# Weight masks between decode steps, earlier exponentials and a regrouped last ten pairs in a convolution and two gated MLPs

## Chip, cores and metric

One core of one Trainium2 chip runs the whole program in one launch. The metric is device microseconds of one execution, lower is better. Before the change the median of 3 executions was 1251.18 us (1250.5 to 1252.2).

## What is computed

The reference, cut to what matters (8192 tokens, width 192, hidden widths 1536 and 2048, all in float32 accuracy):

```python
w = exp(weight_gen - max) / (sum + 1e-9)             # softmax over 7 taps, 8 heads per token
out = einsum('bshk,bskhg->bshg', w, x_unf)           # causal convolution with 7 taps
xn = out / sqrt(mean(out**2) + 1e-6) * rms_g
g = xn @ w_gate                                      # 192 x 1536
y = (g * sigmoid(g) * (xn @ w_val)) @ w_out          # 1536 x 192
h = y @ w_in                                         # 192 x 2048
z = (h * sigmoid(1.702 * h)) @ w_out2                # 2048 x 192
```

## The kernel before, in words

The tokens lie in 16 blocks of 512. Every product is made in three passes, since each operand is split into a high part `h` and a low rest `l` (both fp32r): high by high, high by low, low by high. The matrix rows are cut into an upper and a lower half of 64; two matmuls, one on each half of TensorE, run beside each other as a **pair** (`mm`, L376). Two halves may not write the same bank of PSUM in turn without a hand-over: `handed` (L389) puts a GpSimd nop between them, which waits for the one and is waited for by the other.

The work is a list of **units** (L544). A unit of kind 1, (1, b, m), makes the 128 hidden columns m of the first MLP for block b: `U1` (L455) sends pg and pv through TensorE (9 pairs), then ScalarE makes p = silu(pg) (L463), VectorE p = p * pv (L467), ScalarE h = high part of p (L468), VectorE l = p - h (L471). A unit of kind 2, (2, b, i), makes two slices of the second MLP (`U2`, L474): ScalarE h and p (L484, L485), VectorE l (L491). The down products of a unit (5 pairs per slice, `D1`, `D2`) are put one or two units later, so that h and l are there (`pend`). Four PSUM banks (`pu`) hold pg, pv and ph: a unit can only begin to fill a bank when the unit two before it has been read out of it. Blocks 0 and 1 go first, interleaved, then block by block; the first four units of kind 1 of the next block stand ahead of the eight units of kind 2 of this one. `Y` (L504) splits the first MLP's output for the second, `Z` (L524) scales the sums of the second and stores them.

Beside the units three side works run:

- **Pieces of weights.** 34 pieces (12 w1, 6 wo1, 8 w2, 8 wo2) arrive as 64-bit doubles, each loaded twice (`st`, and `zt` shifted by 16 bits; L87, L88; three buffers of each) and turned into high and low parts by `piece` (L82): x1 on ScalarE (L95), x2 on VectorE: two masks (L99 of st, L101 of zt), then x3, x4, x5 on VectorE (L105, L109, L115), each reading what the one before wrote, then x6, the high part, on ScalarE (L120). `piece_steps` (L592), called 33 times, moves a line of three pieces on: it ends the oldest, does x3 to x5 of the second and x1 and x2 of the third. x5 also calls `load_pieces`, which issues the loads of the piece after next.
- **Softmax.** Seven groups of blocks. `softmax_ops` (L162) gives VectorE operations ahead of the exponential (`pre`), one ScalarE exponential (L186; it needs a table load ahead of it and one behind it, back to silu), and VectorE operations behind it (`post`).
- **Convolution** of a block (`conv_ops`, L216): 13 VectorE operations of 768 columns and some small ones.

The order on every engine is that in which this program calls the operations (a manual schedule); `some` spreads the side works between the units by their estimated cost and due position. Where each group's exponential stands is set at L714 to L727: for group 3 at pos[2, nxt - 2, 2], the third unit of kind 2 of a block, for groups 4 to 6 two units behind `start_at`, that is among units of kind 1. The last two slices' down products (ten pairs) come after the last unit, one slice after the other (L763).

Of the kernel before, what the change touches and what calls it, by code (L numbers as in the profile page):

```python
# [9 lines left out]
F32 = mybir.dt.float32  # L10
# [4 lines left out]
ALU = mybir.AluOpType  # L15
# [3 lines left out]
P = 128  # L19
# [6 lines left out]
DR = D - P  # L26
# [4 lines left out]
BLOCKS = [4] * 16  # L31
# [6 lines left out]
TURN = 5  # L38
SIG = 1.702
# [3 lines left out]
def gated_conv_mlp(ctx: ExitStack, tc: tile.TileContext, xp, wg, w1, wo1, w2, wo2, g, out):  # L43
    nc = tc.nc
    NB = len(BLOCKS)
    T0 = [sum(BLOCKS[:i]) for i in range(NB)]
    TM = max(BLOCKS)
    NM = TM * P
# [33 lines left out]
    def piece(src, high, low):  # L82

        st = stg.tile([P, PC, 2], I32, tag="st", name="st")
        zt = stg.tile([P, PC + 1, 2], I32, tag="zt", name="zt")
        I16 = mybir.dt.int16
        nc.sync.dma_start(out=st.rearrange("p n t -> p (n t)"), in_=src.bitcast(I32))  # L87
        nc.sync.dma_start(out=zt.rearrange("p n t -> p (n t)").bitcast(I16)[:, 1:4 * PC + 1], in_=src.bitcast(I16))  # L88
        t = {}
        hi, mid = st[:, :, 1], zt[:, 0:PC, 1]  # L90

        def x1():
            t["a"] = dec.tile([P, PC], F32, tag="a", name="dec_a")

            nc.scalar.mul(out=t["a"], in_=hi.bitcast(F32), mul=2.0 ** -112)  # L95

        def x2():
            t["s"] = dec.tile([P, PC], I32, tag="s", name="dec_s")
            nc.vector.tensor_scalar(out=t["s"], in0=hi, scalar1=-0x80000000, scalar2=4,  # L99
                                    op0=ALU.bitwise_and, op1=ALU.bitwise_or)  # L100
            nc.vector.tensor_single_scalar(mid, mid, 7, op=ALU.logical_shift_left)  # L101

        def x3():
            ai = t["a"].bitcast(I32)
            nc.vector.scalar_tensor_tensor(out=ai, in0=ai, scalar=3, in1=t["s"],  # L105
                                           op0=ALU.logical_shift_left, op1=ALU.bitwise_or)

        def x4():
            nc.vector.tensor_single_scalar(t["s"], t["a"].bitcast(I32), -0x800000, op=ALU.bitwise_and)  # L109

        def x5():
            v, sf = mid, t["s"].bitcast(F32)
            if len(low.shape) == 3:
                v, sf = (x.rearrange("p (k d) -> p k d", d=D) for x in (v, sf))
            nc.vector.scalar_tensor_tensor(out=low, in0=v, scalar=2.0 ** -43, in1=sf, op0=ALU.mult, op1=ALU.mult)  # L115
            load_pieces()

        def x6():
            for out, of in high:
                nc.scalar.copy(out, of(t["a"]))  # L120
        return [x1, x2], [x3, x4, x5], [x6]

    def piece_up(src, i, nm):

# [251 lines left out]
    def mm(ps, N, rows, w, x, start, stop):  # L376
        def f():
            ins = nc.tensor.matmul(ps[:, :N], w[rows], x[rows, :N], start=start, stop=stop)  # L378
            handed(ins, ps, rows)
        return f  # L380
# [71 lines left out]
            g()  # L452


    def U1(b, m, todo):  # L455
        N = BLOCKS[b] * P
        pg = pu.tile([P, NM], F32, tag="u", name=f"pg{b}_{m}")
        pv = pu.tile([P, NM], F32, tag="u", name=f"pv{b}_{m}")
        todo(((pg, W1[m][0]), (pv, W1[m][1])), N, xT[b])
        p = hid.tile([P, NM], F32, tag="p", name=f"p1_{b}_{m}")  # L460
        h = parts[-1][0].tile([P, NM], F32R, tag="h", name=f"h1_{b}_{m}")
        l = parts[-1][1].tile([P, NM], F32R, tag="l", name=f"l1_{b}_{m}")
        nc.scalar.activation(out=p[:, :N], in_=pg[:, :N], func=AF.Silu)  # L463
        hl1[b, m] = (h, l)

        def second():
            nc.vector.tensor_tensor(out=p[:, :N], in0=p[:, :N], in1=pv[:, :N], op=ALU.mult)  # L467
            nc.scalar.copy(h[:, :N], p[:, :N])  # L468

        def third():  # L470
            nc.vector.tensor_tensor(out=l[:, :N], in0=p[:, :N], in1=h[:, :N].bitcast(F32), op=ALU.subtract)  # L471
        return second, third
# [48 lines left out]
        nc.vector.tensor_tensor(out=sl[:, :N], in0=t[:, :N], in1=sh[:, :N].bitcast(F32), op=ALU.subtract)  # L521
        yT[b] = (h, l, sh, sl)

    def Z(b):  # L524
        N = BLOCKS[b] * P
        pa, pb = acc2.pop(b)
        za = zp.tile([P, NM], F32, tag="za", name=f"za{b}")
        zb = zp.tile([P, NM], F32, tag="zb", name=f"zb{b}")[0:DR]
        order, like = ("p (q j t) -> p q j t", "p (j q t) -> p q j t") if b >= TURN else ("p (j q t) -> p j q t",) * 2

        def of(v, how):
            return v[:, :N].rearrange(how, j=BLOCKS[b], t=Q)
        nc.scalar.mul(out=of(zb, like), in_=of(pb[DR:P], order), mul=1.0 / SIG)
        nc.scalar.mul(out=of(za, like), in_=of(pa, order), mul=1.0 / SIG)
        top, low = of(pb[0:DR], order), of(zb, like)
        for k in range(BLOCKS[b] if b >= TURN else 1):
            z, v = (low[:, :, k], top[:, :, k]) if b >= TURN else (zb[:, :N], pb[0:DR, :N])
            nc.vector.scalar_tensor_tensor(out=z, in0=v, scalar=1.0 / SIG, in1=z, op0=ALU.mult, op1=ALU.add)
        c = T0[b] * P
        nc.sync.dma_start(out=out[0:P, c:c + N], in_=za[:, :N])  # L540
        nc.sync.dma_start(out=out[P:D, c:c + N], in_=zb[:, :N])
# [49 lines left out]

    def piece_steps():  # L592


        for want, r in zip((0, 1, 2), list(line)):
            while len(r) > want:
                for f in r.pop(0):
                    f()
        line.popleft()


# [4 lines left out]
    def add_work(k, end, ops):  # L606
        streams[k].extend((end, c, f) for c, f in ops)
# [30 lines left out]
    pend = deque()  # L638

    with ExitStack() as order:  # L640
# [46 lines left out]
        nxt = 2  # L687
        ex_hook = None
        start_at = pos[1, 1, 2]
        for i, u in enumerate(units):  # L690
            kind, b, m = u
            if (kind, b, m) == (1, 2, 0):
# [17 lines left out]
            if i == start_at:  # L710
                if nxt < 4:
                    load_x(nxt)
                end = xt_at[nxt]
                gi = group_of.get(nxt)  # L714
                if gi is not None and gi >= 2:
                    pr, ex_hook, post_ops = softmax_ops(gi, sm[gi])
                    ex_at = i + 4 if gi == 2 else i + 2 if nxt > TURN else pos[2, nxt - 2, 2]
                    add_work(1, ex_at, pr)
                else:
                    add_work(1, end - 2, conv_ops(nxt))  # L720
                gi = group_of.get(nxt + 1)
                if gi is not None and gi >= 2:
                    sm[gi] = softmax_load(gi)
            if ex_hook and i == ex_at:
                ex_hook()
                ex_hook = None
                add_work(1, xt_at[nxt] - 2, post_ops + conv_ops(nxt))  # L727
            downs, after = [], []
            while pend and pend[0][0] <= i:
                _, D_, key = pend.popleft()  # L730
# [27 lines left out]
            else:  # L758
# [1 line left out]
                last = len(units) - 1  # L760
                pend.append((i + 2 if b > 1 and m == 0 else i + 1, D2, (b, 2 * m)))
                pend.append((i + 1 if b < 2 or i + 1 == last else i + 2, D2, (b, 2 * m + 1)))
        while pend:  # L763
            _, D_, key = pend.popleft()
            d, f = D_(*key)
            matmuls(None, [d])
            if f:
                f()


# [47 lines left out]
```

## Time and profile before

| | before |
|---|---|
| median of 3 executions | 1251.18 us (1250.5 to 1252.2) |
| the profiled execution, its own time | 1251.86 us |
| its span | 1250.1 us, 26884 instructions |
| TensorE matmul busy | 1221.5 us, 98% |
| TensorE weight load busy | 1109.7 us, 89% |
| VectorE busy | 778.2 us, 62% |
| ScalarE busy | 651.1 us, 52% |
| GpSimd busy | 32.1 us, 3% |
| granted TensorE clock | 0.997 of full speed (2.4 GHz) |

Times are from the start of the span. A matmul's end is modelled, so TensorE's busy share overstates what it does; the start of one unit's first matmul against the next unit's tells more. A row of the timeline names the start, the duration, engine, line, operation, what it writes and reads, and in brackets how long the engine was idle before it and what ended that. Durations of neighbours on VectorE overlap somewhat: the start of one to the start of the next is what it takes on the engine.

### The profile page before, as it was taken

The numbers are of one execution on the slowest core, as the hardware profiler recorded it, in microseconds if no ns is written. First come the engines' busy times: TensorE is split into PE (matmuls) and PEld (weight loads), VectorE is DVE, ScalarE is ACT, GpSimd is POOL, SyncE is SP. The second block draws the span as 40 slices with busy tenths as digits, with TensorE's granted clock in tenths as the row PEclk, the third lists the DMA queues.
The fourth block names the chain that finished last, engine by engine and source line by source line (L and its number), as shares of the span: only waits on it lengthen the run. The fifth ranks groups of instructions, "written<-read, shape, count | busy, mean of one in ns | idle before, by whom it ended". The sixth has DMA issues, their size and how long they took to land.

```text
span 1250.1 us, 26884 instructions
## 1 busy us (share of the span) xinstructions
PE 1221.5 (98%) x10324; PEld 1109.7 (89%) x10324; DVE 778.2 (62%) x1292; ACT 651.1 (52%) x1279; POOL 32.1 (3%) x53
## 2 busy tenths in 40 slices
PE   6998999999999999999999999999999999999998
PEld 3776899888888989999988999999899999889996
DVE  8989947576657375664747657475674746545432
ACT  4565664554545455454555545455554554544553
POOL 4000000000000000000000000000000000000000
PEclk9999999999999999999999999999999999999999
DMA  5855511001001000100111001010110001000000
GB/s 185 262 175 167 164 56 45 2 1 46 33 14 54 11 27 33 31 33 11 33 33 31 33 14 49 7 38 33 31 33 11 22 33 31 1 17 16 1 14 14
DMA packets 33856, 57.52 MB, mean 46 GB/s; under 512 B 7744, under 2 KB 19392, under 8 KB 33728
## 3 DMA queue, kind: packets, MB, share of 16 engines
q1 hardware_dynamic: 33728, 55.80, 14.4%
q8 instruction: 82, 1.34, 0.5%
q14 instruction: 46, 0.38, 0.1%
HBM read 43.71 MB, written 6.29 MB: 40 GB/s over the span
## 4 chain that ended last, share of the span: by engine, by line
PE 87%; DVE 8%; ACT 3%; issue 1%; DMA 0%; POOL 0%; SPq 0%; DVEq 0%; POOLq 0%; ACTq 0%
PE a L378 24%; PE ph L378 21%; PE b L378 15%; PE pg L378 15%; PE pv L378 13%; DVE p L467 1%; DVE l L471 1%; DVE dec_a L105 1%; DVE xr L227 1%; DVE dec_s L109 1%; DVE dec_s L99 1%; DMA x<-in_xp 0%; DVE zt L101 0%; ACT L463 0%; ACT h L468 0%
## 5 line engine op out<-in xcount | busy, mean ns | idle before, releaser
L378 PE MATMUL a<-h,o 64*128 64x512 f32 x1792 | 518.9, 392 | 0.4 <-POOLq L393 0.2
L378 PEld LDWEIGHTS a<-h,o 64*128 64x128 f32 x1792 | 328.4, 184 | 15.2 <-POOLq L393 1.1
L491 DVE TENSOR_TENSOR l<-p,h 128x512 fp32r<-128x512 f32 x256 | 176.5, 691 | 226.3 <-ACT p L485 226.0
L378 PE MATMUL a<-l,o 64*128 64x512 f32 x896 | 311.1, 392 | 1.5 <-DVE l L491 1.3
L378 PE MATMUL b<-l,o 64*128 64x512 f32 x896 | 311.0, 392 | 0.3 <-DVE l L471 0.3
L378 PE MATMUL b<-h,o 64*128 64x512 f32 x896 | 311.0, 393 | 0.0
L484 ACT ACTIVATE h<-ph 128x512 fp32r<-128x512 f32 x256 | 153.8, 601 | 219.7 <-PE ph L378 212.7
L378 PE MATMUL pv<-xh,w 64*128 64x512 f32 x768 | 242.1, 395 | 4.5 <-DVE p L467 4.1
L378 PE MATMUL pg<-xh,w 64*128 64x512 f32 x768 | 244.1, 395 | 2.4 <-ACT w L120 2.0
L378 PE MATMUL ph<-yh,w 64*128 64x512 f32 x1024 | 237.7, 392 | 1.8 <-DVE p L467 1.7
L468 ACT CAST h<-p 128x512 fp32r<-128x512 f32 x192 | 119.3, 621 | 190.4 <-DVE p L467 190.4
L467 DVE TENSOR_TENSOR p<-p,pv 128x512 f32<-128x512 f32 x192 | 131.7, 686 | 112.6 <-PE a L378 87.5
L463 ACT ACTIVATE p<-pg 128x512 f32<-128x512 f32 x192 | 114.6, 597 | 157.2 <-PE pg L378 152.6
L471 DVE TENSOR_TENSOR l<-p,h 128x512 fp32r<-128x512 f32 x192 | 132.4, 690 | 71.6 <-ACT h L468 71.3
L378 PEld LDWEIGHTS a<-l,o 64*128 64x128 f32 x896 | 165.5, 185 | 11.7 <-DVE l L491 3.0
L378 PEld LDWEIGHTS b<-l,o 64*128 64x128 f32 x896 | 165.6, 185 | 8.6 <-DVE l L471 1.0
L378 PEld LDWEIGHTS b<-h,o 64*128 64x128 f32 x896 | 164.1, 185 | 7.5 <-ACT h L484 0.4
L378 PEld LDWEIGHTS ph<-yh,w 64*128 64x128 f32 x1024 | 146.9, 185 | 13.9 <-DVE p L467 2.4
L378 PEld LDWEIGHTS pv<-xh,w 64*128 64x128 f32 x768 | 140.1, 185 | 16.4 <-DVE p L467 8.6
L378 PE MATMUL ph<-yl,w 64*128 64x512 f32 x512 | 154.0, 391 | 0.0
L485 ACT ACTIVATE p<-ph 128x512 f32<-128x512 f32 x256 | 153.6, 600 | 0.1
L378 PEld LDWEIGHTS pg<-xh,w 64*128 64x128 f32 x768 | 140.6, 185 | 11.4 <-ACT w L120 2.9
(110 smaller groups left out, 2113.7 us busy)
## 6 DMA issues: line engine op xcount, KB each, us to landing
x<-in_xp SPq DMA_DIRECT2D x15, 960.0 KB, 4.8
st<-in_w SPq DMA_DIRECT2D x20, 384.0 KB, 3.9
zt<-in_w SPq DMA_DIRECT2D x20, 384.0 KB, 3.4
st<-in_wo SPq DMA_DIRECT2D x14, 384.0 KB, 3.9
zt<-in_wo SPq DMA_DIRECT2D x14, 384.0 KB, 3.4
out_z<-za SPq DMA_DIRECT2D x16, 256.0 KB, 2.2
xl<-raw SPq DMA_DIRECT2D x176, 16.0 KB, 1.8
xsl<-raw SPq DMA_DIRECT2D x176, 16.0 KB, 1.8
```

What stands on the lines that cost most here:

```text
L99: nc.vector.tensor_scalar(out=t["s"], in0=hi, scalar1=-0x80000000, scalar2=4, op0=ALU.bitwise_and, op1=ALU.bitwise_or)
L105: nc.vector.scalar_tensor_tensor(out=ai, in0=ai, scalar=3, in1=t["s"], op0=ALU.logical_shift_left, op1=ALU.bitwise_or)
L109: nc.vector.tensor_single_scalar(t["s"], t["a"].bitcast(I32), -0x800000, op=ALU.bitwise_and)
L227: eng.tensor_tensor(out=dst.rearrange("p (q g) -> p q g", g=GRP), in0=x[:, (k + j0) * D:(k + j1) * D].rearrange("p (q g) -> p q g", g=GRP) ...
L378: ins = nc.tensor.matmul(ps[:, :N], w[rows], x[rows, :N], start=start, stop=stop)
L463: nc.scalar.activation(out=p[:, :N], in_=pg[:, :N], func=AF.Silu)
L467: nc.vector.tensor_tensor(out=p[:, :N], in0=p[:, :N], in1=pv[:, :N], op=ALU.mult)
L468: nc.scalar.copy(h[:, :N], p[:, :N])
L471: nc.vector.tensor_tensor(out=l[:, :N], in0=p[:, :N], in1=h[:, :N].bitcast(F32), op=ALU.subtract)
L484: nc.scalar.activation(out=h[:, :N], in_=ps[j][:, :N], func=AF.Silu, scale=SIG)
L485: nc.scalar.activation(out=p[:, :N], in_=ps[j][:, :N], func=AF.Silu, scale=SIG)
L491: nc.vector.tensor_tensor(out=l[:, :N], in0=p[:, :N], in1=h[:, :N].bitcast(F32), op=ALU.subtract)
```

## The change

Three edits.

1. x2 is split: the mask of zt becomes a step of its own, x2m. `piece_steps` first ends the oldest piece and calls x1 of the newest, then alternates x3, x4, x5 of the middle piece with the two masks of the newest: x3, mask of st, x4, mask of zt, x5.
2. For groups 4 to 6 `pre` and the exponential are taken one block earlier: `pre` beside the convolution of the block before, the exponential at pos[2, nxt - 2, 2], the third unit of kind 2, `post` with the next block's convolution. Their load of the raw weights goes one block earlier on the sync queue.
3. The last ten pairs become one function, `last_downs`. The lower half of the sums a gets a bank of its own (`a2_own`), the halves are ordered anew, and `Z` adds the extra bank with four more VectorE operations; ScalarE scales a before b.

```diff
@@ -98,6 +98,8 @@
             t["s"] = dec.tile([P, PC], I32, tag="s", name="dec_s")
             nc.vector.tensor_scalar(out=t["s"], in0=hi, scalar1=-0x80000000, scalar2=4,
                                     op0=ALU.bitwise_and, op1=ALU.bitwise_or)
+
+        def x2m():
             nc.vector.tensor_single_scalar(mid, mid, 7, op=ALU.logical_shift_left)
 
         def x3():
@@ -118,7 +120,7 @@
         def x6():
             for out, of in high:
                 nc.scalar.copy(out, of(t["a"]))
-        return [x1, x2], [x3, x4, x5], [x6]
+        return [x1, x2, x2m], [x3, x4, x5], [x6]
 
     def piece_up(src, i, nm):
 
@@ -452,6 +454,26 @@
             g()
 
 
+    def last_downs(tiles):
+
+        accs, own = tiles[0][0], pacc.tile([P, NM], F32, tag=f"a{NB % 2}", name="a2_own")
+        N = tiles[0][5]
+        upper, lower = [], []
+        for n, (_, a, b, _, _, _) in enumerate(tiles):
+            end = n == len(tiles) - 1
+            a, b = a[0] + a[1], b[0] + b[1]
+            upper += [[mm(accs[0], N, UPPER, w, x, False, end and i == len(a) - 1) for i, (w, x) in enumerate(a)],
+                      [mm(accs[1], N, UPPER, w, x, False, end and i == len(b) - 1) for i, (w, x) in enumerate(b)]]
+            lower += [[mm(own, N, LOWER, w, x, n == 0 and i == 0, end and i == len(a) - 1) for i, (w, x) in enumerate(a)],
+                      [mm(accs[1], N, LOWER, w, x, False, False) for w, x in b]]
+        (a0, b0), (a1, b1) = lower[:2], lower[2:]
+        upper = upper[0] + upper[2] + upper[1] + upper[3]
+        lower = b0 + b1[:1] + a0[:1] + b1[1:] + a0[1:] + a1
+        for f, g in zip(upper, lower, strict=True):
+            f()
+            g()
+        return own
+
     def U1(b, m, todo):
         N = BLOCKS[b] * P
         pg = pu.tile([P, NM], F32, tag="u", name=f"pg{b}_{m}")
@@ -521,7 +543,7 @@
         nc.vector.tensor_tensor(out=sl[:, :N], in0=t[:, :N], in1=sh[:, :N].bitcast(F32), op=ALU.subtract)
         yT[b] = (h, l, sh, sl)
 
-    def Z(b):
+    def Z(b, own=None):
         N = BLOCKS[b] * P
         pa, pb = acc2.pop(b)
         za = zp.tile([P, NM], F32, tag="za", name=f"za{b}")
@@ -530,8 +552,16 @@
 
         def of(v, how):
             return v[:, :N].rearrange(how, j=BLOCKS[b], t=Q)
-        nc.scalar.mul(out=of(zb, like), in_=of(pb[DR:P], order), mul=1.0 / SIG)
-        nc.scalar.mul(out=of(za, like), in_=of(pa, order), mul=1.0 / SIG)
+        if own is None:
+            nc.scalar.mul(out=of(zb, like), in_=of(pb[DR:P], order), mul=1.0 / SIG)
+            nc.scalar.mul(out=of(za, like), in_=of(pa, order), mul=1.0 / SIG)
+        else:
+            nc.scalar.mul(out=of(za, like), in_=of(pa, order), mul=1.0 / SIG)
+            nc.scalar.mul(out=of(zb, like), in_=of(pb[DR:P], order), mul=1.0 / SIG)
+            for k in range(BLOCKS[b]):
+                z = of(za, like)[:, :, k]
+                nc.vector.scalar_tensor_tensor(out=z, in0=of(own, order)[:, :, k], scalar=1.0 / SIG, in1=z,
+                                               op0=ALU.mult, op1=ALU.add)
         top, low = of(pb[0:DR], order), of(zb, like)
         for k in range(BLOCKS[b] if b >= TURN else 1):
             z, v = (low[:, :, k], top[:, :, k]) if b >= TURN else (zb[:, :N], pb[0:DR, :N])
@@ -591,11 +621,20 @@
 
     def piece_steps():
 
-
+        runs = []
         for want, r in zip((0, 1, 2), list(line)):
+            runs.append([])
             while len(r) > want:
-                for f in r.pop(0):
-                    f()
+                runs[-1] += r.pop(0)
+        last, mid, first = (runs + [[], []])[:3]
+        masks, rest = first[-2:], first[:-2]
+        for f in last + rest + mid[:-3]:
+            f()
+        mid = mid[-3:]
+        while mid or masks:
+            for q in (mid, masks):
+                if q:
+                    q.pop(0)()
         line.popleft()
 
 
@@ -687,6 +726,7 @@
         nxt = 2
         ex_hook = None
         start_at = pos[1, 1, 2]
+        soft = {}
         for i, u in enumerate(units):
             kind, b, m = u
             if (kind, b, m) == (1, 2, 0):
@@ -712,19 +752,27 @@
                     load_x(nxt)
                 end = xt_at[nxt]
                 gi = group_of.get(nxt)
-                if gi is not None and gi >= 2:
+                if gi in soft:
+                    add_work(1, end - 2, soft.pop(gi) + conv_ops(nxt))
+                elif gi is not None and gi >= 2:
                     pr, ex_hook, post_ops = softmax_ops(gi, sm[gi])
-                    ex_at = i + 4 if gi == 2 else i + 2 if nxt > TURN else pos[2, nxt - 2, 2]
+                    ex_at = i + 4 if gi == 2 else pos[2, nxt - 2, 2]
                     add_work(1, ex_at, pr)
                 else:
+                    gi = group_of.get(nxt + 1)
+                    if gi is not None and gi >= 4:
+                        pr, ex_hook, soft[gi] = softmax_ops(gi, sm[gi])
+                        ex_at = pos[2, nxt - 2, 2]
+                        add_work(1, ex_at, pr)
                     add_work(1, end - 2, conv_ops(nxt))
-                gi = group_of.get(nxt + 1)
-                if gi is not None and gi >= 2:
+                gi = group_of.get(nxt + (1 if nxt < 4 else 2))
+                if gi is not None and gi >= 2 and gi not in sm:
                     sm[gi] = softmax_load(gi)
             if ex_hook and i == ex_at:
                 ex_hook()
                 ex_hook = None
-                add_work(1, xt_at[nxt] - 2, post_ops + conv_ops(nxt))
+                if group_of.get(nxt) not in (None, *soft):
+                    add_work(1, xt_at[nxt] - 2, post_ops + conv_ops(nxt))
             downs, after = [], []
             while pend and pend[0][0] <= i:
                 _, D_, key = pend.popleft()
@@ -760,12 +808,8 @@
                 last = len(units) - 1
                 pend.append((i + 2 if b > 1 and m == 0 else i + 1, D2, (b, 2 * m)))
                 pend.append((i + 1 if b < 2 or i + 1 == last else i + 2, D2, (b, 2 * m + 1)))
-        while pend:
-            _, D_, key = pend.popleft()
-            d, f = D_(*key)
-            matmuls(None, [d])
-            if f:
-                f()
+        tiles = [down_halves(*D2(*key)[0]) for _, _, key in pend]
+        Z(NB - 1, last_downs(tiles))
 
 
 # ---- launch: one core; host code lays data out only ----
```

Where instructions now stand, at three places. VectorE, the step that makes the low part of w1's piece 3, with its neighbours, before (dec_a and dec_s are scratch tiles, w_3 is what TensorE reads, p_1_0 and l_1_0 are of unit (1, 1, 0)):

```order
L467 TENSOR_TENSOR p_1_0_470<-p_1_0_470,pv_0_437 128x512
L105 SCALAR_TENSOR_TENSOR dec_a<-dec_a,dec_s 128x384
L109 TENSOR_SCALAR dec_s<-dec_a 128x384
L115 SCALAR_TENSOR_TENSOR w_3_319<-zt,dec_s 128x384
L99 TENSOR_SCALAR dec_s<-st 128x384
L101 TENSOR_SCALAR zt<-zt 128x384
L471 TENSOR_TENSOR l_1_0_472<-p_1_0_470,h_1_0_471 128x512
```

and the same step now:

```order
L489 TENSOR_TENSOR p_1_0_470<-p_1_0_470,pv_0_437 128x512
L107 SCALAR_TENSOR_TENSOR dec_a<-dec_a,dec_s 128x384
L99 TENSOR_SCALAR dec_s<-st 128x384
L111 TENSOR_SCALAR dec_s<-dec_a 128x384
L103 TENSOR_SCALAR zt<-zt 128x384
L117 SCALAR_TENSOR_TENSOR w_3_319<-zt,dec_s 128x384
L493 TENSOR_TENSOR l_1_0_472<-p_1_0_470,h_1_0_471 128x512
```

The same five operations stand between p and l; no two that depend on each other are neighbours any more. The same holds for 31 steps.

ScalarE, the exponential of group 4, before (zb, za are the output of block 4, p_5_6 is of unit (1, 5, 6)):

```order
L468 CAST h_5_5_6334<-p_5_5_6333 128x512
L533 ACTIVATE zb_6342<-b_4_5835 64x512
L534 ACTIVATE za_6341<-a_4_5834 128x512
L186 ACT_TABLE_LOAD
L186 ACTIVATE wraw_5177<-wraw_5177 128x672
L463 ACT_TABLE_LOAD
L463 ACTIVATE p_5_6_6390<-pg_6_6354 128x512
```

and now (h_4_3 and h_4_4 are of the units (2, 4, 1) and (2, 4, 2)):

```order
L506 ACTIVATE h_4_3_5831<-ph_3_5790 128x512
L507 ACTIVATE p_4_3_5830<-ph_3_5790 128x512
L188 ACT_TABLE_LOAD
L188 ACTIVATE wraw_4378<-wraw_4378 128x672
L506 ACT_TABLE_LOAD
L506 ACTIVATE h_4_4_5897<-ph_4_5842 128x512
```

It left the units of kind 1 behind a block's output for a unit of kind 2, eight units earlier; groups 5 and 6 likewise.

TensorE, part of the last ten pairs before (h_15_14 to l_15_15 are the last two slices):

```order
L378 MATMUL a_15_17397<-l_15_14_17755,o_2203 128x512
L378 MATMUL a_15_17397<-h_15_14_17754,o_2203 128x512
L378 MATMUL b_15_17398<-h_15_14_17754,o_2203 128x512
L378 MATMUL a_15_17397<-h_15_14_17754,o_2203 128x512
L378 MATMUL b_15_17398<-l_15_14_17755,o_2203 128x512
L378 MATMUL a_15_17397<-l_15_14_17755,o_2203 128x512
L378 MATMUL a_15_17397<-h_15_15_17759,o_2203 128x512
```

and now, from the seventh of the twenty on:

```order
L380 MATMUL a_15_17397<-h_15_15_17759,o_2208 128x512
L380 MATMUL a_own<-h_15_14_17754,o_2208 128x512
L380 MATMUL a_15_17397<-h_15_15_17759,o_2208 128x512
L380 MATMUL b_15_17398<-l_15_15_17760,o_2208 128x512
L380 MATMUL a_15_17397<-l_15_15_17760,o_2208 128x512
L380 MATMUL a_own<-h_15_14_17754,o_2208 128x512
L380 MATMUL b_15_17398<-h_15_14_17754,o_2208 128x512
L380 MATMUL a_own<-l_15_14_17755,o_2208 128x512
```

Where a was written by both halves in turn, the lower half now writes a_own; only b still goes from the lower to the upper half, once, with two other matmuls between.

## Rows read from the trace of the kernel before

**Rows 1.** Busy time by engine, one stretch (length, PE, PEld, DVE, ACT, POOL):

```profile
72.00:115.00 43.00, 39.81 (x323) 29.99 (x319) 39.73 (x83) 22.92 (x49) 0.00 (x0) 1.00 0.60 187
```

**Rows 2.** Waits of TensorE, 35 to 140 us (total, times, longest):

```profile
PE pv L378 <- DVE p L467: 3.5, 7, 0.6
```

**Rows 3.** Chain that ended last, 28 to 100 us, shares by line:

```profile
by line: DVE p L467 15.1%; DVE l L471 14.2%; issue 13.0%; DVE dec_a L105 11.3%; DVE dec_s L109 8.8%; DVE dec_s L99 8.4%; DVE zt L101 6.5%; ACT h L468 5.1%; DVE w L115 2.0%; DVE o L115 1.9%; ACT L463 1.8%; DVE xr L282 1.6%; ACT xr L285 1.3%;
```

**Rows 4.** Timeline of VectorE, one step of the pieces:

```profile
101.68 0.55 DVE L105 SCALAR_TENSOR_TENSOR dec_a<-dec_a,dec_s 128x384 int32<-128x384 int32 x1
102.27 0.36 DVE L109 TENSOR_SCALAR dec_s<-dec_a 128x384 int32<-128x384 int32 x1
102.67 0.56 DVE L115 SCALAR_TENSOR_TENSOR w<-zt,dec_s 128x384 fp32r<-128x384 int32 x1
103.14 0.35 DVE L99 TENSOR_SCALAR dec_s<-st 128x384 int32<-128x384 int32 x1
103.41 0.35 DVE L101 TENSOR_SCALAR zt<-zt 128x384 int32<-128x384 int32 x1
103.68 0.68 DVE L467 TENSOR_TENSOR p<-p,pv 128x512 f32<-128x512 f32 x1
```

**Rows 5.** VectorE by line, 30 to 139 us (busy, mean ns, idle before):

```profile
L105 DVE SCALAR_TENSOR_TENSOR dec_a<-dec_a,dec_s 128x384 int32<-128x384 int32 x26 | 14.4, 553 | 0.0
```

**Rows 6.** Timelines of ScalarE and VectorE, unit (1, 0, 3):

```profile
48.68 0.61 ACT L463 ACTIVATE p<-pg 128x512 f32<-128x512 f32 x1
...
49.77 0.67 DVE L467 TENSOR_TENSOR p<-p,pv 128x512 f32<-128x512 f32 x1
```

**Rows 7.** Timeline of VectorE, two places where it waits for ScalarE:

```profile
69.55 0.69 DVE L467 TENSOR_TENSOR p<-p,pv 128x512 f32<-128x512 f32 x1 [1.12 <-ACT p L463]
...
130.13 0.69 DVE L518 TENSOR_TENSOR yt<-yt,b 128x512 f32<-128x512 f32 x1 [0.63 <-ACT yt L516]
```

**Rows 8.** Timeline of TensorE, first matmuls of units of kind 1, undisturbed and at group 4:

```profile
209.69 0.39 PE L378 MATMUL pg<-xh,w 64*128 64x512 f32 x1
...
216.23 0.39 PE L378 MATMUL pg<-xh,w 64*128 64x512 f32 x1
...
440.50 0.39 PE L378 MATMUL pg<-xh,w 64*128 64x512 f32 x1
...
447.96 0.39 PE L378 MATMUL pg<-xh,w 64*128 64x512 f32 x1
```

**Rows 9.** Group 3's exponential (ScalarE) and first matmuls of units of kind 2:

```profile
254.18 1.28 ACT L186 ACT_TABLE_LOAD   x1
...
258.17 0.63 PE L378 MATMUL ph<-yh,w 64*128 64x512 f32 x4
...
262.58 0.63 PE L378 MATMUL ph<-yh,w 64*128 64x512 f32 x4
...
267.00 0.62 PE L378 MATMUL ph<-yh,w 64*128 64x512 f32 x4
```

**Rows 10.** Timeline of all engines, the last ten microseconds:

```profile
1240.28 0.40 PE L378 MATMUL a<-h,o 64*128 64x512 f32 x1
...
1240.75 0.39 PE L378 MATMUL a<-l,o 64*128 64x512 f32 x1
...
1241.25 0.49 PE L378 MATMUL a<-h,o 64*128 64x512 f32 x1
...
1243.86 0.39 PE L378 MATMUL b<-l,o 64*128 64x512 f32 x1
...
1244.29 0.59 ACT L533 ACTIVATE zb<-b 64x512 f32<-64x512 f32 x1 [4.10 <-PE b L378]
...
1244.91 0.87 DVE L538 SCALAR_TENSOR_TENSOR zb<-b,zb 64x128 f32<-64x128 f32 x4 [4.00 <-ACT zb L533]
...
1245.97 1.21 SPq L541 DMA_DIRECT2D out_z<-zb  x1
```

**Rows 11.** Loads of zt (L88): one issue, the mask of its piece, landings of all:

```profile
36.55 0.33 SPq L88 DMA_DIRECT2D zt<-in_w  x1
...
42.50 0.35 DVE L101 TENSOR_SCALAR zt<-zt 128x384 int32<-128x384 int32 x1
...
DMA to landing us min/median/max: 3.1/3.4/8.4
```

## The prediction

> **What bounds the kernel now.** I first read the busy shares by stage, then who waits for whom, then the chain that ended last, then the timelines at the places that the edits touch. For most of the span TensorE is the bound: in undisturbed stretches a unit of kind 1 follows the last after (216.23 - 209.69) / 2 = 3.27 us [rows 8] and one of kind 2 after 4.42 us [rows 9], and no edit changes that work. Time can only come from places where TensorE waits. There are three kinds. From about 30 to 138 us, while the weights are decoded, VectorE is busy 39.73 of 43 us [rows 1], TensorE waits for VectorE's p [rows 2], and the chain runs through VectorE's lines: the four decode lines L105, L109, L99 and L101 alone hold 35% of it, TensorE hardly any [rows 3]. At the exponentials of groups 4 to 6 two units take 447.96 - 440.50 = 7.46 us instead of 6.54 [rows 8], a loss of 0.92 us each. In the last ten pairs TensorE is held by the hand-overs between the halves [rows 10].
>
> **Edit 1, the masks.** The step [rows 4] shows what an operation costs by its neighbour. L105 to L109, which reads its result, is 102.27 - 101.68 = 0.59 us; L115, of the same kind and size, lets an independent L99 begin after 103.14 - 102.67 = 0.47. L109 to the dependent L115 is 0.40; the masks, of the same kind as L109, let the next one begin after 0.27. So a dependent neighbour begins only when the one before has ended, an independent one about 0.1 us sooner. Before: 0.59 + 0.40 + 0.47 + 0.27 + 0.27 = 2.00 us. Now every neighbour is independent, and by the time L109 and L115 are reached (0.47 + 0.27 = 0.74 and 0.27 + 0.27 = 0.54 behind what they read, against 0.59 and 0.40 needed) their inputs are there: 0.47 + 0.27 + 0.27 + 0.27 + 0.47 = 1.76. I take 0.235 us per step.
>
> How much of it is on the path? 26 steps begin between 30 and 139 us [rows 5]; the last of them comes after the chain has passed to TensorE, so 25 count, 5.9 us at most. Three lie under another wait: the step ahead of 69.55, where VectorE then idles 1.12 us for group 2's exponential, and the two ahead of 130.13, where it idles 0.63 us for the copies of `Y`, which come out of TensorE [rows 7]. That leaves 22 x 0.235 = 5.2. Early on VectorE can't keep its whole lead: its p needs ScalarE's silu of the same unit, which needs TensorE. At 49.77 the silu had ended at 48.68 + 0.61 = 49.29 [rows 6], so 0.48 us of lead can be used, and what TensorE itself has gained by then: the two first steps stand ahead of its inputs, 0.24 to 0.47, I take 0.37. Six steps have won 1.41 there and keep 0.85, so 0.56 is lost. From 72 us on VectorE has well over TensorE's 3.27 us of work per unit (below), and I count nothing more as lost. **Term 1: 5.2 - 0.6 = 4.6 us**, bounds 5.9 (all 25) and 3.4 (the cap costs three times as much).
>
> The queues: VectorE's low part (L115) now ends 0.3 us later in its step, and x6, which follows a step later, and TensorE don't need it before; the load of zt behind it starts 0.3 us later. A mask that now waits for a load would hold L115 and p and l behind it. The tightest place: issued at 36.55, landed after the median 3.4, at 39.95, read at 42.50 [rows 11], 2.55 us to spare. The mask moves up within its step by 1.73 - 1.01 = 0.72, the release moves back by 0.30, and two shorter steps take 0.47: 1.06 us stay. I cost that at nothing.
>
> Here a rule speaks against the edit. The rows show that a dependent neighbour costs 0.11 to 0.13 us more than an independent one [rows 4]. The Trainium skill, VectorE: DVE Perf Modes, section "The DRAIN you can't avoid", says that the next operation does not start before the pipe has emptied and that chaining without semaphores doesn't skip it, which would leave the order of the five without effect; the same section adds that an operation that is not held starts earlier. By the first half of it term 1 would be 0; the trace bears out the second.
>
> **Edit 2, the exponentials.** They leave units of kind 1, where each costs 0.92 us, for the third unit of kind 2. Group 3's already stands there: its table load begins at 254.18, and the next units of kind 2 start at 258.17, 262.58 and 267.00, 4.41 and 4.42 us apart, the undisturbed pace [rows 9]. The new places have the same units around them, so I cost the exponential there at nothing; its cover is ScalarE's free time in two units of kind 2. `pre` and `post` are as many operations as before, spread over more units, on a VectorE that is 62% busy; three loads of raw weights move up the sync queue past a shuffle, far from their use. **Term 2: 3 x 0.92 = 2.8 us**, bounds 2.8 and 2.3 (a sixth of the stall stays).
>
> **Edit 3, the last ten pairs.** The first starts at 1240.28. A hand-over takes 1241.25 - 1240.75 = 0.50 us, where a pair takes (1240.75 - 1240.28) / 2 = 0.23, and the last b starts at 1243.86 [rows 10]. Of three hand-overs one stays, with two other matmuls between: the lower b starts at about 1241.21, may be handed on at 1241.71, and its follower is due at 1241.68. I add 0.15 for that and the refill behind it. The last pair then starts at 1240.28 + 9 x 0.233 + 0.15 = 1242.52, and what reads it 1244.29 - 1243.86 = 0.43 later, at 1242.95. From there the old tail was ScalarE's scaling and then four VectorE operations of 0.87 us together; now ScalarE's b runs beside four new operations on a, and the four on b follow: 2 x 0.87 = 1.74, so b is ready at 1244.7 where it was ready at 1244.91 + 0.87 = 1245.78. **Term 3: 1.1 us**, bounds 0.5 (a full hand-over and refill more) and 1.9 (the store of b, 1.21 us in its issue [rows 10] so close behind that of a, loses two thirds of it).
>
> **Sum.** 4.6 + 2.8 + 1.1 = 8.5 us. From the profiled execution's 1251.86 that gives 1243.4; that execution stands 0.7 over the median of 1251.18, so for the median I forecast **1242.7 us**. With all bounds together 10.6 to 6.2 us, that is 1240.6 to 1245.0.
>
> **The rivals.**
> - *The cap holds all along.* If the silu limits p in every unit as it does at 49.77, term 1 is the 0.85 of there and two or three steps more, 1.4 us: 1251.2 - 5.3 = 1245.9. For it: 0.48 us is small. Against it: in 72 to 115 us VectorE is busy 92% [rows 1], and 323 matmuls at 28 to a unit are 11.5 units of 3.73 us, where TensorE needs 3.27.
> - *The pipe empties all the same.* Term 1 is 0: 1251.2 - 3.9 = 1247.3. That is the skill's rule above; rows 4 speak against it, unless the 0.1 us come from something else that the new neighbours share.
> - *The exponential takes its stall along.* Term 2 is 0: 1245.5. Against it, rows 9.
> - *Slower: the masks wait for their loads.* Between the end of one L115 and the mask of the piece three on lie two steps of length T less 0.84 us. With 3.4 us to land, T may fall to 2.1; but the longest landing seen is 8.4 [rows 11]. Steps of 3.5 us (one to a unit at most, 3.73 less 0.235) would stretch once every landing takes over 6.1 us, and the kernel would be slower than before by more than 2.5 us once it takes 7.1. At 7.5 T is 4.18, and 24 steps grow by 0.68 each, 16.4 us: 1251.2 - 8.5 + 16.4 = 1259.1. Only the loads at the start and those beside a block of x take so long.
>
> **Chances.** The forecast 0.74; the cap 0.10; the pipe 0.07; the exponential 0.05; the loads 0.04. About 0.2%, 2.5 us, is what a measurement of this kernel can tell from no change. The first four are all faster by more than that but for a tail; half of the last is within it: faster 0.95, same 0.03, slower 0.02. The range holds the forecast's own and reaches to the cap and the exponential: 1240.6 to 1246.0; left out are the pipe, the loads and what of the forecast errs beyond its bounds.
>
> **What would show it.** Right: L105 to the next L99 0.47 us, the five operations 1.76 us, and group 3's table load, at 254.18 before [rows 9], 4 to 5 us earlier; block 5's units 7 and 8 at 3.27 us each, and no wait of TensorE around the moved exponentials; one wait for GpSimd in the last ten pairs. Wrong: steps still of 2.0 us, idle time of VectorE ahead of its masks ended by a DMA, new idle time ahead of p ended by the silu between 40 and 115 us, or units of kind 2 behind a moved exponential that take more than 4.42 us.

## Result, and the profile after

The changed kernel takes 1240.74 us (median of 4 executions, 1240.47 to 1241.27), the kernel before, measured beside it, 1251.15 us (4 executions, 1250.5 to 1252.2). The ratio is 0.9917 [0.9902, 0.9932]: 10.4 us faster, where 8.5 were forecast. The profiled execution took 1240.54 us with a span of 1238.6, 11.5 us less than the span before.

The page of the changed kernel, from its parts 1 and 4 (busy time; the chain that ended last):

```profile
PE 1215.7 (98%) x10324; PEld 1100.3 (89%) x10324; DVE 773.1 (62%) x1296; ACT 650.2 (52%) x1279; POOL 32.3 (3%) x53
...
PE 90%; DVE 7%; ACT 2%; issue 1%; DMA 0%; POOL 0%; DVEq 0%; POOLq 0%; ACTq 0%
```

and part 4 of the kernel before:

```profile
PE 87%; DVE 8%; ACT 3%; issue 1%; DMA 0%; POOL 0%; SPq 0%; DVEq 0%; POOLq 0%; ACTq 0%
```

Busy time hardly moved, and TensorE is busy for 98% as before: what went is time in which it waited. The starts of the units, unit by unit in both traces, say where. The first matmul of unit (2, 1, 0), where the weight stage is over, stood at 138.29 us and now stands here (timeline of TensorE, changed kernel):

```profile
132.56 0.39 PE L380 MATMUL ph<-yh,w 64*128 64x512 f32 x1
```

That is 5.73 us, 0.28 of which were there before the first unit began. At the old places of the exponentials of groups 4, 5 and 6, from unit 7 to unit 9 of blocks 5, 8 and 11, the starts move apart by 0.95, 0.94 and 0.95, 2.8 us together. From the last unit to the end it is 1.87. The remaining 1.1 us came in steps of about 0.1 us along the way.

**The step** (timeline of VectorE, changed kernel; [rows 4] have it before):

```profile
97.19 0.55 DVE L107 SCALAR_TENSOR_TENSOR dec_a<-dec_a,dec_s 128x384 int32<-128x384 int32 x1
97.66 0.36 DVE L99 TENSOR_SCALAR dec_s<-st 128x384 int32<-128x384 int32 x1
97.94 0.35 DVE L111 TENSOR_SCALAR dec_s<-dec_a 128x384 int32<-128x384 int32 x1
98.20 0.35 DVE L103 TENSOR_SCALAR zt<-zt 128x384 int32<-128x384 int32 x1
98.47 0.55 DVE L117 SCALAR_TENSOR_TENSOR w<-zt,dec_s 128x384 fp32r<-128x384 int32 x1
98.94 0.68 DVE L489 TENSOR_TENSOR p<-p,pv 128x512 f32<-128x512 f32 x1
```

The five operations last as long as before, 0.55 and 0.35 us, but each begins 0.47 or 0.27 us behind its neighbour: 98.94 - 97.19 = 1.75 us instead of 2.00.

**The weight stage is still VectorE's.** Busy time by engine in a stretch of it (length, PE, PEld, DVE, ACT, POOL), changed kernel:

```profile
72.00:110.00 38.00, 36.93 (x303) 28.25 (x301) 35.20 (x75) 21.94 (x47) 0.00 (x0) 1.00 0.64 197
```

VectorE is busy 35.20 of 38.00 us, 93%, the 92% of [rows 1] once more. Who waits for whom, 35 to 135 us, changed kernel, for VectorE (us, times, longest):

```profile
DVE l L493 <- ACT h L490: 4.3, 7, 0.7
...
DVE p L489 <- ACT p L485: 1.4, 1, 1.4
```

and for TensorE:

```profile
PE pv L380 <- DVE p L489: 1.1, 5, 0.3
```

TensorE's wait of pv for p fell from 3.5 us [rows 2] to 1.1. No idle time of VectorE is ended by a DMA, and the only one ahead of p ended by the silu is that at group 2's exponential. New ground for an experiment is the first row: seven times VectorE stands idle between p and l.

**The exponentials.** Group 3's, which [rows 9] show before, and group 4's in its new place (timeline of ScalarE), with the starts of the units of kind 2 behind group 3's (TensorE), changed kernel:

```profile
248.41 1.28 ACT L188 ACT_TABLE_LOAD   x1
...
252.41 0.64 PE L380 MATMUL ph<-yh,w 64*128 64x512 f32 x4
...
256.84 0.63 PE L380 MATMUL ph<-yh,w 64*128 64x512 f32 x4
...
261.26 0.63 PE L380 MATMUL ph<-yh,w 64*128 64x512 f32 x4
...
397.81 1.28 ACT L188 ACT_TABLE_LOAD   x1
399.10 0.77 ACT L188 ACTIVATE wraw<-wraw 128x672 f32<-128x672 f32 x1
399.89 1.28 ACT L506 ACT_TABLE_LOAD   x1
401.18 0.60 ACT L506 ACTIVATE h<-ph 128x512 fp32r<-128x512 f32 x1
```

The units keep their 4.42 us, and where two units of kind 1 took 7.46 us [rows 8], units (1, 5, 7) to (1, 5, 9) now take 441.31 - 434.80 = 6.51:

```profile
434.80 0.39 PE L380 MATMUL pg<-xh,w 64*128 64x512 f32 x1
...
441.31 0.39 PE L380 MATMUL pg<-xh,w 64*128 64x512 f32 x1
```

From 140 to 1226 us no wait of TensorE's matmuls is left in the list of waits.

**The end** (timeline of all engines, changed kernel; [rows 10] before):

```profile
1230.71 0.39 PE L380 MATMUL b<-h,o 64*128 64x512 f32 x1
...
1231.64 0.39 PE L380 MATMUL b<-l,o 64*128 64x512 f32 x1
...
1231.91 0.39 PE L380 MATMUL a<-l,o 64*128 64x512 f32 x1
1232.21 0.50 PE L380 MATMUL b<-h,o 64*128 64x512 f32 x1
...
1233.02 0.39 PE L380 MATMUL b<-l,o 64*128 64x512 f32 x1
...
1234.34 0.87 DVE L568 SCALAR_TENSOR_TENSOR zb<-b,zb 64x128 f32<-64x128 f32 x4
...
1235.28 0.47 SPq L571 DMA_DIRECT2D out_z<-zb  x1
```

One hand-over is left (1231.64 to 1232.21), and it costs 1232.21 - 1231.91 = 0.30 where a pair takes 0.23. The last store's issue takes 0.47 us, not the 1.21 of [rows 10].

### The profile page after: what moved, and what is told of

It reads as the page before. It is cut to its first block, busy times and chain, and to the rows that moved or that the text cites. A ratio compares the mean times of both kernels' runs of the same rounds, so it can differ in the third digit from the quotient of the medians.

```text
span 1238.6 us, 26868 instructions
## 1 busy us (share of the span) xinstructions
PE 1215.7 (98%) x10324; PEld 1100.3 (89%) x10324; DVE 773.1 (62%) x1296; ACT 650.2 (52%) x1279; POOL 32.3 (3%) x53
## 4 chain that ended last, share of the span: by engine, by line
PE 90%; DVE 7%; ACT 2%; issue 1%; DMA 0%; POOL 0%; DVEq 0%; POOLq 0%; ACTq 0%
PE a L380 24%; PE ph L380 21%; PE b L380 16%; PE pv L380 14%; PE pg L380 14%; DVE p L489 1%; DVE l L493 1%; DVE xr L229 1%; DVE dec_a L107 1%; ACT h L490 0%; DVE w L117 0%; DVE dec_s L99 0%; DVE dec_s L111 0%; DVE o L117 0%; DVE acc L262 0%
## 5 line engine op out<-in xcount | busy, mean ns | idle before, releaser
L380 PE MATMUL ph<-yh,w 64*128 64x512 f32 x1024 | 234.4, 392 | 1.6 <-DVE p L489 1.4
L380 PE MATMUL ph<-yl,w 64*128 64x512 f32 x512 | 151.2, 391 | 0.0
L380 PE MATMUL pv<-xl,w 64*128 64x512 f32 x384 | 150.5, 392 | 0.0
```

## Experiments

The theory: three separate gains. The masks take 0.25 us off each step because no operation stands behind the one that it reads from; the exponentials leave their 0.92 us behind; the end loses its hand-overs. Rivals: what counts is only that the masks moved; the three gains share one cover and don't add up; the loads are the next bound.

### Each edit alone

**e1_masks** has edit 1 alone (`x2m` and the new `piece_steps`), **e2_exps** edit 2 alone (the planner's lines from `soft` on), **e3_tail** edit 3 alone (`last_downs` and `Z`); **e0_before** is the kernel before once more, profiled in a single execution (1250.67 us).

> Edit 1 alone. If the whole gain of the early stretch comes from the five decode operations no longer waiting for their neighbour (2.00 to 1.75 us a step), block 1's first unit of kind 2 starts 5.2 to 5.7 us earlier than before and the time is 5.2 to 5.7 us lower, about 1245.7 us. If the pipe emptied all the same, 1251.2; if the silu capped the lead everywhere, 1249.8.

> Edit 2 alone. Theory: three stalls of 0.92 us vanish and nothing else moves, 1248.3 us. If the exponentials take a stall along to the units of kind 2, 1251.2 or more. If the extra softmax work beside a convolution holds TensorE elsewhere, more than 1248.8 with waits of TensorE for p or l between 250 and 1230 us.

> Edit 3 alone. If its worth is only that b is ready sooner (1.0 us between the first of the last pairs and the last VectorE operation), 1250.1 us. If the short issue of the last store (0.47 us instead of 1.21) is its doing too, 1249.4 us and that issue is again near 0.47 us.

> The kernel before, profiled once more. If the 1.21 us issue of the last store belongs to its order of work, it is again about 1.2 us; if it was that one execution's, it is near 0.5 us and the span about 0.7 us shorter. The stretch from 140 to 1230 us shows how much the pace of TensorE differs between two executions: theory 0.5 to 1 us.

| | us (range) | ratio to before [95%] | gain |
|---|---|---|---|
| before, beside them (18 executions) | 1250.99 (1250.40 to 1251.85) | | |
| edit 1 alone | 1245.22 (1244.91 to 1246.55) | 0.9956 [0.9943, 0.9968] | 5.8 |
| edit 2 alone | 1247.57 (1247.33 to 1248.08) | 0.9972 [0.9962, 0.9982] | 3.4 |
| edit 3 alone | 1249.87 (1249.31 to 1250.50) | 0.9991 [0.9982, 1.0000] | 1.1 |

The gains add up to 10.3 us, the 10.4 of the change: no shared cover. The interval of edit 3 reaches 1.0000, so its time alone does not set it apart from no change; the traces below do. Against the second trace of the kernel before, edit 1 has 5.43 us of its gain by unit (2, 1, 0), and edit 2 has 0.90, 0.92 and 0.96 at the three old places, 2.8 of its 3.4 (2.3 to 4.8 by its interval); the other half microsecond again came in steps of 0.1. Two traces of the same kernel before differ by as much (0.38 us ahead of the first unit, 0.6 up to the last), so steps of that size are no effect that a single trace can show. The ends differ too: the second trace of the kernel before issues its last store so (timeline of the sync queue):

```profile
1245.41 0.47 SPq L541 DMA_DIRECT2D out_z<-zb  x1
```

The 1.21 us of [rows 10] belonged to one execution (0.47 in each of the other traces); no edit has to explain it. Against this second trace the stretch from the last unit to the end is 1.3 us shorter, in the changed kernel and with edit 3 alone: that, and 1.1 by the medians, is edit 3's.

### Where the masks stand

**e4_pair** is the changed kernel with both masks between x3 and x4, **e5_first** with both ahead of x3 (each has one of the two `for` lines):

```diff
-        while mid or masks:
-            for q in (mid, masks):
-                if q:
-                    q.pop(0)()
+        for f in mid[:1] + masks + mid[1:]:      # e4_pair
+        for f in masks + mid:                    # e5_first
+            f()
```

> The changed kernel with both masks between x3 and x4, so that x4 and x5 are dependent neighbours again. Theory (a dependent neighbour costs 0.12 to 0.13 us): a step of 1.87 us, half of edit 1's gain lost, 1240.7 + 2.7 = 1243.4 us. If what counts is only that the masks come ahead of x5, no difference, 1240.7.

> The changed kernel with both masks ahead of x3, so that x3, x4 and x5 are neighbours as before the change. Theory: a step of 2.0 us, all of edit 1's gain lost, 1246.2 us. If early masks were what helped, 1240.7 or less. If early masks wait for their loads, more than 1246.2 with idle time of VectorE ended by DMAs.

e4_pair took 1244.38 us (1244.25 to 1245.65; ratio 0.9946 [0.9932, 0.9959] to 1251.45 for the kernel before beside it), e5_first 1247.25 (1246.59 to 1247.38; 0.9966 [0.9954, 0.9979]), each 1.0 us more than I had expected. The step of e4_pair (timeline of VectorE):

```profile
91.82 0.55 DVE L107 SCALAR_TENSOR_TENSOR dec_a<-dec_a,dec_s 128x384 int32<-128x384 int32 x1
...
92.83 0.35 DVE L111 TENSOR_SCALAR dec_s<-dec_a 128x384 int32<-128x384 int32 x1
93.22 0.56 DVE L117 SCALAR_TENSOR_TENSOR w<-zt,dec_s 128x384 fp32r<-128x384 int32 x1
93.69 0.68 DVE L489 TENSOR_TENSOR p<-p,pv 128x512 f32<-128x512 f32 x1
```

and that of e5_first:

```profile
93.35 0.35 DVE L99 TENSOR_SCALAR dec_s<-st 128x384 int32<-128x384 int32 x1
...
95.34 0.68 DVE L489 TENSOR_TENSOR p<-p,pv 128x512 f32<-128x512 f32 x1
```

In e4_pair one dependent pair is left, L111 to L117, and it takes 0.39 us instead of 0.27; the step is 1.87 us. In e5_first both pairs are left and the step is 1.99 us. So the time of a step is the sum over its neighbours, 1.75, 1.87 and 1.99 us, and the kernel's time follows: 1240.7, 1244.4 and 1247.3. By unit (2, 1, 0) the two stand 2.66 and 5.42 us behind the changed kernel (less 0.34 that e4_pair began late), which is 22 x 0.12 and 22 x 0.245; the one more microsecond that the medians show comes further on, in steps too small to place. Nor do the masks of e5_first wait for their loads, the rival of its expectation: between 25 and 140 us no idle time of VectorE is ended by a DMA. With all of edit 1 but its order, nothing of its gain is left: 1251.4 less the 3.4 and 1.1 of the other edits is 1246.9.

What holds the reader back stands in the trace as well: L109 and L115 of the kernel before each carry a wait for the semaphore that VectorE's own instructions raise, and begin 0.03 us after their neighbour has ended; the masks carry no such wait. L111 and L117 of the changed kernel carry it too, but begin 0.27 us behind a mask, since by then what they read is done. No run takes that wait away, so whether the engine would hold a reader without it stays open. The Trainium skill, VectorE: DVE Perf Modes, section "The DRAIN you can't avoid", says both that the next operation waits until the pipe has emptied, which chaining without semaphores can't skip, and that an operation which is not held starts earlier. These three orders refute the first for operations that don't read what their neighbour wrote (0.27 us to the next, of 0.35), and bear out the second.

### The loads as the next bound

The slower rival needed loads that come too late. **e6_two_after** and **e7_two_before** take one of the three load buffers away, in the changed kernel and in the one before:

```diff
-NST = 3
+NST = 2
```

> The changed kernel with two buffers for the raw weights instead of three. Theory: the load of zt is issued at the end of one L117 and read 1.01 us into the next step, so a step can't take less than 0.03 + 3.4 + 1.84 - 1.01 = 4.3 us and VectorE waits for DMAs ahead of its masks; about 0.6 to 0.8 us in each of some 24 steps, 1255 to 1260 us, slower than the kernel before. If loads are far off the path, 1240.7.

> The kernel before with two buffers for the raw weights. Theory: the mask stands 1.73 us into the step and the load is issued 1.54 us into the one before, so a step may fall to 3.2 us and hardly waits: 1251 to 1253 us. If two buffers hold up any order of the step, 1260 or more.

e6_two_after took 1257.36 us (1256.04 to 1257.94; ratio 1.0047 [1.0033, 1.0060]), as expected, e7_two_before 1254.27 (1253.28 to 1256.40; 1.0025 [1.0014, 1.0035]), over the 1251 to 1253 I had expected. Waits of VectorE, 25 to 140 us, in e6_two_after:

```profile
DVE zt L103 <- DMA zt<-in_w: 7.5, 8, 1.7
DVE zt L103 <- DMA zt<-in_wo: 6.0, 8, 1.7
```

and in e7_two_before, where the waits for DMAs come to 2.4 us in all:

```profile
DVE zt L101 <- DMA zt<-in_w: 1.0, 2, 0.6
```

With two buffers the same change makes the kernel 3.1 us slower. In the traces e6_two_after stands 5.8 us behind e7_two_before by unit (2, 1, 0) and wins 4.2 back from there on, where edits 2 and 3 act: moving the masks up costs 5.8 us there (7.6 by the medians, if those edits give their full 4.5), since 16 masks now wait for their loads and hold L117, p and l behind them. The rival's mechanism is real; three buffers keep it hidden. How narrowly, the changed kernel shows at the thirteenth load of zt (sync queue and VectorE):

```profile
50.84 0.42 SPq L214 DMA_DIRECT2D x<-in_xp  x1
...
52.80 0.33 SPq L88 DMA_DIRECT2D zt<-in_w  x1
...
60.28 0.36 DVE L103 TENSOR_SCALAR zt<-zt 128x384 int32<-128x384 int32 x1
```

Issued behind a block of x, it landed after 7.04 us, at 59.85 in the trace, 0.44 us ahead of its mask. How long this one load takes differs between executions of the same kernel: 5.79 and 7.75 us in the two traces of the kernel before (margins 3.19 and 1.24), 7.04 and 5.71 in the two of the changed kernel (0.44 and 1.69; the second is f0_after below). At nearly equal landings, 5.79 and 5.71, the change took 1.5 us of the margin. With the 7.75 of the kernel before, the mask of the changed kernel would have waited about 0.3 us (an estimate: 60.28 - 52.80 = 7.48 are there).

### Filling VectorE's idle times

In the changed kernel VectorE stands idle seven times between p and l, waiting 0.6 to 0.7 us for ScalarE's h, 4.3 us in all. **f1_fill** lets `some` say whether it did anything; where it did nothing between p and l of a unit of kind 1 of blocks 0 and 1, one operation is taken from the side work (a piece's step where no other was left). **f0_after** is the changed kernel again. The place where `fill` is called, without its own lines and those in `some`:

```diff
-                some(todo)
+                if not some(todo) and kind == 1 and b < 2:
+                    fill()
                 third()
```

> The changed kernel again, beside the next one on the same chip: 1240.7 us, as before. Its execution also shows how much the start of units drifts between two executions of one program.

> The changed kernel, in which VectorE takes one small operation of the softmax or the convolution forward where it would otherwise stand idle between p and l of a unit (seven times 0.6 to 0.7 us, 4.3 us in all, ended by ScalarE's h). Theory that VectorE is still the bound there: the idle time is filled, and the weight stage ends 2 to 4 us earlier, 1237 to 1239 us. Rival, that those idle times lie where TensorE limits the units anyway: 1240.7, no change. Second rival, that the operation taken forward is longer than the idle time and holds l, which the down products wait for: 1241 to 1243 us, with a new wait of TensorE for l.

f0_after took 1240.77 us (1240.48 to 1241.66), f1_fill 1240.45 (1240.37 to 1241.04; ratios to before 0.9918 [0.9904, 0.9931] and 0.9917 [0.9903, 0.9931]): no difference, where I had expected 1237 to 1239. Yet the idle time was filled (0.3 us are left of the 4.3), and by unit (2, 0, 1) f1_fill had won 2.3 us on f0_after, not counting the 0.88 that it was ahead at the first unit; the rest shows as a longer wait of VectorE at group 2's exponential, 3.0 us instead of 1.4. It lost 1.9 of them by unit (2, 1, 3), with new waits of TensorE (its timeline, f1_fill):

```profile
117.97 0.50 PE L380 MATMUL a<-l,o 64*128 64x512 f32 x1 [0.92 <-DVE l L513]
...
147.65 0.49 PE L380 MATMUL a<-l,o 64*128 64x512 f32 x1 [0.70 <-DVE l L513]
```

There TensorE needs the l of units of kind 2, whose first share of side work stands ahead of both l and whose second stands between them; with a step or a convolution operation between, the second l comes too late for the down products, which for blocks 0 and 1 are only one unit later. **f2_fill_late** therefore also takes both l ahead of the second share; **f3_late** does that alone:

```diff
                 second()
-                some(todo)
-                third()
+                if kind == 2 and b < 2:
+                    third()
+                    some(todo)
+                else:
+                    some(todo)
+                    third()
```

> The filled idle times of the run before, and in the units of kind 2 of blocks 0 and 1 both low parts l ahead of the second share of side work instead of one on each side. Theory that the 2 us won by 113 us were given back only because a step or a convolution operation stood between the two l and made TensorE wait (0.92 us at 117.97, 0.70 at 147.65): 1238.5 to 1239.5 us, without those waits. Rival, that TensorE is the bound from 110 us on whatever stands there, and holds the gain at the pace of its units: 1240.5 us.

> The changed kernel with the second edit of the run beside it alone (both l together in the units of kind 2 of blocks 0 and 1). Its waits of TensorE for l are 0.8 us in all: 1240.2 to 1240.8 us by either theory; more only if side work now comes later than its place needs.

f2_fill_late took 1236.40 us (1235.95 to 1236.63; ratio to before 0.9882 [0.9865, 0.9898]), f3_late 1240.51 (1240.47 to 1242.04; 0.9918 [0.9903, 0.9933]). Waits of TensorE in f2_fill_late, 30 to 165 us:

```profile
PE ph L380 <- DVE p L489: 1.2, 2, 0.9
PE pg L380 <- ACT w L122: 1.0, 1, 1.0
PE pv L380 <- DVE p L489: 0.5, 2, 0.3
```

No wait for l is left, and the gain stays: unit (2, 1, 0) starts at 128.06 us, 4.5 earlier than in the changed kernel. Each edit alone is worth nothing (0.3 us, and none), both together 4.0: 14.4 us below the kernel before beside them, against 10.4. I had expected 1238.5 to 1239.5, the 2.3 us won by 113 us kept; from (2, 0, 1) to (2, 1, 0) f2_fill_late wins another 2.15 on the changed kernel. About as much lay in the changed kernel itself, in a row that I had passed over since it is that of the weight loads (waits, 115 to 133 us, changed kernel; the wait for l stands at the load ahead of the matmul that reads it, and shows there more than at the matmul):

```profile
PEld a L380 <- DVE l L513: 2.5, 4, 0.9
```

In f2_fill_late no weight load waits for l from 112.6 to 128.1 us. In f3_late, where VectorE has not got ahead by filling its idle time, 1.6 us of such waits stay, and nothing is won, though 0.9 us of them are gone: that these waits are the 2.15 us is argued from the sizes, not shown. f2_fill_late is the fastest version here.

## Why the prediction was right, and where not

**What bounds the kernel**: right. The chain's share of TensorE rose from 87 to 90%, all the gain of size came out of waits, and out of the three places named.

**Edit 1, 4.6 forecast, 5.4 to 5.8 measured.** The steps took 0.25 us less each, not 0.235, and the count of 22 held: 22 x 0.25 = 5.5. What failed is the deduction of 0.56 for the cap at 49.77: "Early on VectorE can't keep its whole lead". In the changed kernel that p begins at 48.00 (timelines of ScalarE, TensorE and VectorE):

```profile
45.75 0.62 ACT L490 CAST h<-p 128x512 fp32r<-128x512 f32 x1 [0.96 <-DVE p L489]
46.28 0.51 ACT L122 CAST w<-dec_a 128x384 fp32r<-128x384 f32 x1
46.69 0.57 ACT L95 ACTIVATE dec_a<-st 128x384 f32<-128x384 f32 x1
...
46.93 0.39 PE L380 MATMUL pg<-xl,w 64*128 64x512 f32 x1
...
47.37 0.60 ACT L485 ACTIVATE p<-pg 128x512 f32<-128x512 f32 x1
...
48.00 0.69 DVE L489 TENSOR_TENSOR p<-p,pv 128x512 f32<-128x512 f32 x1
```

It is 1.77 us earlier than in [rows 6], less 0.28 that the execution was ahead: all of 6 x 0.25. I had tied the silu to TensorE. In the trace before, the last matmul of its pg and ScalarE's queue read (timelines of ScalarE and TensorE):

```profile
47.28 0.62 ACT L468 CAST h<-p 128x512 fp32r<-128x512 f32 x1 [1.22 <-DVE p L467]
...
47.76 0.39 PE L378 MATMUL pg<-xl,w 64*128 64x512 f32 x1
...
48.22 0.58 ACT L95 ACTIVATE dec_a<-st 128x384 f32<-128x384 f32 x1
```

So pg was complete at 48.15, and the silu began only at 48.68: it stood in ScalarE's queue right behind h, the high part of the weights and L95, and h waits for VectorE's p of the unit before. As VectorE came earlier, so did that queue, and the silu had another 0.53 us to move up before TensorE could hold it. That slack is missing in the prediction. In the changed kernel it is used up: pg is complete at 47.32, the silu begins 0.05 us later and 0.11 after L95 has ended. It moved up by 1.31 us and pg by 0.83, the slack of 0.48 shrank to 0.03, and no lead was lost; but at this place little more could have been won.

**The loads**: hidden, as forecast, and at the place I named the margin is 1.13 us (forecast 1.06). But it was not the tightest: behind the block of x 0.44 was left in one execution and 1.69 in another. I had taken the median landing for the smallest margin, though I knew of landings of 8.4 us at the start; the longest landing just ahead of a step decides. That the loads stayed hidden there is in part luck, since the landing at this place varied by 2 us.

**Edit 2, 2.8 forecast, 2.8 measured** at the three places, 3.4 in the medians, over the bound of 2.8 but within what the measurement can tell. The new places cost nothing: behind each of the three the units of kind 2 keep 4.41 to 4.43 us.

**Edit 3, 1.1 forecast, 1.1 measured** by the medians, 1.3 by the traces. The last pair starts 2.31 us after the first of the ten (forecast 2.24), b is ready at 1235.21, 4.50 us after it (forecast 4.4). The hand-over and the refill behind it cost 0.21 instead of 0.15. The upper bound of 1.9 rested on the 1.21 us of the last store's issue, which was that execution's own.

**The sum** came out 1.9 us short: 0.8 to 1.2 are edit 1's, about 0.5 is edit 2's half microsecond without a place, and the two medians of the kernel before agree within 0.03. The measured 1240.74 lies only 0.1 us inside the lower end of the range. That end is in part luck: it adds 5.9 for edit 1, with all 25 steps, and 1.9 for edit 3, which rested on the odd 1.21 us of one store. Group 3's table load moved 5.77 us (0.28 of them the execution's lead) where I had written 4 to 5, for the same reason as term 1. The rivals fell: the silu cap by 48.00, the emptying pipe by the step, the exponential's stall by the 4.42 us behind it, the loads by VectorE's waits.

## What to carry to other kernels

On an engine that sets the pace, cost an operation by the start of its neighbour, and put an independent operation between a writer and its reader; here that took 12% off a step of five without removing any work. Before deducting something for an input that "can't come earlier", follow its producer's own queue to see what released it: if that is the engine being sped up, the input comes earlier too, as far as what it is made from is ready. When an engine's idle time is filled and nothing comes of it, look a stage further for the wait that took the gain back; the two edits that are worth nothing alone were worth 4.0 us together.

## What the runs showed of the hardware

- On VectorE, an operation that reads what the one before wrote begins 0.11 to 0.13 us later than one that doesn't (0.59 against 0.47 us behind L105, 0.39 against 0.27 behind a mask of 128x384). That an independent operation between them hides all of it, at no cost of its own, I had assumed; the step's 1.75 us show it.
- Moving ScalarE's tables for an exponential takes 1.28 us each way, and the next activation begins 0.01 us later (397.81 + 1.28 to 399.10; 399.89 + 1.28 to 401.18): a switch there and back costs 2.6 us of ScalarE, which two units of kind 2 hide.
- Loads of zt, all of the same size, landed after 3.1 to 4.1 us in the two traces of the changed kernel, but for the first three (6.8 to 8.5), the last (5.0 and 5.1) and the one issued behind a block of x on the same queue (7.0 and 5.7). The same load in the same kernel before took 5.8 us in one execution and 7.75 in the other.
